# Attention and feed-forward on one core: third batch by DMA, other group cuts, x and output stores moved to GpSimd

## The chip, the cores and the metric

The kernel runs on one core of one Trainium2 chip. The metric is the device time of a launch in microseconds (us), as the median of several runs. Engines are called PE (TensorE matmul; PEld is its weight load), DVE (VectorE), ACT (ScalarE), POOL (GpSimd) and SP (SyncE). A letter q after a name (SPq, ACTq) means the engine's sequencer, which issues DMAs.

## What is computed

The inputs are q, k and v of 8 batches, 8 heads, 576 positions and 64 values a head, and two weight matrices.

```python
rel = pos[:, None] - pos[None, :]
mask_plain = (rel >= 0) & (rel < 32)
mask_dil = (rel >= 0) & (rel < 128) & (rel % 4 == 0)
# heads 0-3 take mask_plain, heads 4-7 take mask_dil
attn = softmax(where(mask, q @ k.T / 8, -1e9))
x = (attn @ v) as [4608 tokens, 512]     # tokens in the order batch, position
h = x @ w_in                             # 512 -> 2048
out = (h * sigmoid(h)) @ w_out           # 2048 -> 512, float32
```

## The kernel before, in words

The two weight matrices stay in SBUF as float16. The two layers go through the 4608 tokens in groups: two of 256 tokens, then eight of 512. **Layer 1** (`layer1`, L892 to L905) is 16 steps a group, one for each 128 rows of the hidden layer: four matmuls into a PSUM tile h, a tanh on ACT (th, L901), and the gate on DVE (gT, L903). **Layer 2** (`layer2`, L925 to L946) makes four steps of four matmuls for each 128 tokens into a PSUM tile y; ACT copies y to an output tile ob (L938, two buffers), and the ACT queue stores it (L939). The last 128 tokens are split in two, with one piece stored from SP (L946).

**Attention** works batch by batch. Scores (`scores`, L620 and L632) are computed transposed, by blocks of queries and a band of keys, exponentiated on ACT (L641, L645) and masked on DVE (L650). In the first batch the mask is added by matmuls against the identity (L620). `av` (L677 to L681) multiplies by v, with a column of ones that gives the sum, and DVE divides.

Scores need k and q with the head's 64 values on the partitions. There are two ways to that.

- *PE path*, batches 0 to 2 (`PEB = 3`): raw k and q are loaded from POOL's queue, cast to float16 on the way (nat; `issue_first`, `issue_nat` L124), and transposed on PE (L544, L521, L535; for batch 0 L557, L567, L582, L594). For batches 1 and 2, DVE or ACT first pairs the heads (`paired`, L652), and both copy the results out of PSUM (L510, L512).
- *DMA path*, batches 3 to 7: POOL issues a cast of k and of q into a DRAM scratch (kq_s, `issue_cast` L141), and SP issues four DMA transposes from it (`issue_turn`): two of the plain heads into nat (L155) and two of the dilated heads into kqT (L158). The plain ones read overlapping windows: 2304 rows of 128 values, one row at each step of 64, so that each value comes twice.

v is loaded from POOL too: vraw for dilated heads (two DMAs, L165) and vp for plain ones (one DMA of many small rows, L178).

The result x is needed transposed as well. For batches 0 to 2 (`PEX = 3`) PE transposes it into xA (L722, L733). For later batches SP stores it to a DRAM scratch x_s, in four DMAs a batch (oP L696, oD L715), and then transposes a whole group by DMA into xA or one of three rotating tiles xR (L450). Which group waits for which batch is in `need`: the batch of the group's last token.

**The order of the work** is fixed when the program is built. The class `Plan` holds a clock, the time at which each engine comes free, and rings of PSUM tiles. A loop (L990 on) takes at each moment a step that the plan holds ready, from three lists: attention, layer 1, layer 2. Layer 1 may be at most one group ahead of layer 2. What a step costs on an engine and when loads land (`AT_...`, `LOAD_US`, the numbers in the `yield` lines) are constants by hand. Every engine runs its own instructions in the order in which they were emitted.

`loads_gen` (L424 to L438) emits a batch's loads of the DMA path. POOL first copies one column of the previous batch's kqT (fence, L427), and, from batch 5 on, one of the x of two batches before (L429); each copy waits for that transpose to land. Then come vraw, vp and the casts. `turn_gen` emits the four transposes, `group_gen` the one of x, when all four stores of a batch are out (`stored`).

At the start, loads leave POOL in the order of `ORDER`: k0 and r0 are the rest of batch 0's k, q and v, v0 its plain v, w0a to w3 pieces of w_in, o0 to o3 pieces of w_out, d1, p1, r1, v1 the loads of batch 1 (dilated and plain k and q, vraw, vp). `third_batch` then emits raw loads of batch 2, its v, and the casts of batch 3. Eight matmuls of zeros (L192) run first on PE.

Of the kernel before, what the change touches and what calls it, by code (L numbers as in the profile page):

```python
# [16 lines left out]
def kernel(  # L17
# [9 lines left out]
    nc = tc.nc  # L27
# [17 lines left out]
    GROUPS = [(0, GT // 2), (GT // 2, GT // 2)] + [(t, GT) for t in range(GT, NT, GT)]  # L45
# [4 lines left out]
    PEB = 3  # L50
    PEX = 3
    GA = 4
    XR = 3
    NA = GA * GT
    BIG = 32768.0
    ORDER = "k0 r0 w0b v0 w0a w1 w2 w3 d1 p1 o0 r1 o1 o2 o3 v1".split()
    LOAD_US = {"w": 2.57, "o": 2.57, "d": 3.2, "p": 3.0, "r": 2.3, "v": 2.57, "k0": 2.2, "r0": 1.0, "v0": 2.3, "w0a": 1.3, "w0b": 1.3}
    AT_W0 = 11.4
# [18 lines left out]
    xA = cpool.tile([P, HP, GA * GT], F16, name="xA")  # L77
# [13 lines left out]
    NW = HN * S  # L91
# [7 lines left out]
        key: cpool.tile([MA, HP // 2, DIL, 2, D], F16, name=f"pair_{key}")  # L99
        for key in ("k", "q", "rest")  # L100
# [38 lines left out]
    def issue_cast(b):  # L139
        for i, src in enumerate((k, q)):  # L140
            nc.gpsimd.dma_start(  # L141
                out=kq_s[b][i].rearrange("(n p c) -> p n c", c=512, p=144),
                in_=src[b].rearrange("h s d -> (h s d)").rearrange("(n p c) -> p n c", c=512, p=144),
            )

    def issue_turn(b, n):
        i = n % 2
        flat = kq_s[b][i]
        if n < 2:
            if b < PEB + 2 and i == 0:  # L150
                nc.gpsimd.memset(kq_plain(b)[0][:, :LEAD], 0.0)
            win = bass.AP(tensor=flat.tensor, offset=flat.offset, ap=[[D, NW], [1, P]])
            dst = kq_plain(b)[i]
            dst = dst[:, LEAD:] if i == 0 else dst
            nc.sync.dma_start_transpose(out=dst[:, None, :], in_=win)  # L155
        else:
            rows = flat[HN * S * D :].rearrange("(n c) -> n c", c=DIL * D)
            nc.sync.dma_start_transpose(out=kqTs[b % 2][:, i], in_=rows)  # L158
# [29 lines left out]
    warm = vraws[1].rearrange("p a h r d -> p (a h r d)")  # L188
    nc.vector.memset(warm[:, :GT], 0.0)
    y_warm = ps_y.tile([P, GT], F32, tag="y", name="y_warm")  # L190
    for n in range(8):
        nc.tensor.matmul(y_warm, warm[:, :P], warm[:, :GT], start=True, stop=True)  # L192
    nc.vector.memset(warm[:, GT:], 0.0)
# [67 lines left out]
    def third_batch():  # L261
        for n in range(2, PEB):
            issue_nat(n, 0, H)
        issue_vraw(2)
        issue_vp(2)
        issue_cast(PEB)
        yield "DMA", 0.0
# [12 lines left out]
    class Plan:  # L280
        def __init__(self):
# [3 lines left out]
            self.free = {"ACT": 5.7, "DVE": 6.6}  # L285
# [75 lines left out]
    AT_DIL = {0: 6.1, 1: AT["d1"], 2: t2 + 7.0}  # L361
    AT_PLAIN = {0: 9.3, 1: AT["p1"], 2: t2 + 7.0}
    AT_VRAW = {0: 10.1, 1: AT["r1"], 2: t2 + 8.6}
    AT_VP = {0: 11.4, 1: AT["v1"], 2: t2 + 11.4}
    AT_CAST = t2 + 18.0
# [37 lines left out]
    turned = {b: Step(None, 0.0) for b in range(PEB, B)}  # L403
    groups = {g: Step(None, 0.0) for g in range(NG)}

    def x_of(g):
        t0, n = GROUPS[g]
        return xA[:, :, t0 : t0 + n] if t0 < NA else xRs[g % XR]

    def turn_gen(b):  # L410
        for n, us in enumerate((3.0, 3.0, 1.5, 7.5)):
            issue_turn(b, n)
            yield "DMA", us
# [7 lines left out]
    def start_turn(b):  # L421
        plan.push(turned[b], turn_gen(b), plan.now)

    def loads_gen(b):  # L424
        last = max(b - 1, PEB)
        for i in range(2):
            nc.gpsimd.tensor_copy(fence[:, i : i + 1], kqTs[last % 2][:, i, 1, HN * M - 1 :])  # L427
        if b - 2 >= PEX:
            nc.gpsimd.tensor_copy(fence[:, 2:3], x_of(first_of[b - 2])[:, HP - 1, GT - 1 :])  # L429
# [4 lines left out]
        yield "DMA", 9.0  # L434
        v_in[b].done = plan.now
        if b > PEB:
            yield "DMA", 4.5
# [9 lines left out]
    def group_gen(g):  # L447
        t0 = max(GROUPS[g][0], PEX * S)
        n = sum(GROUPS[g]) - t0
        nc.sync.dma_start_transpose(  # L450
            out=x_of(g)[:, :, GT - n :], in_=x_s[t0 : t0 + n]
        )
        yield "DMA", 6.0
        b = need[g]
        if g == first_of[b] and b + 2 < B:
# [10 lines left out]
    def attention(b):  # L466
# [21 lines left out]
        def k_plain(i, hp, j):  # L488
# [3 lines left out]
            c = LEAD + (2 * hp + i) * S + QB * j - W - i  # L492
            return kW[r, c : c + P]

        def q_plain(i, hp, j):
# [3 lines left out]
            c = (2 * hp + i) * S + QB * j - i  # L499
# [185 lines left out]
        def av_p(ring, j):  # L685
# [7 lines left out]
            if not pe_x and parts[j // 3] == 3:  # L693
                j = j // 3 * 3 + 2
                rows = x_s[b * S : (b + 1) * S, : HN * D].rearrange("(j p) c -> p j c", p=QB)
                nc.sync.dma_start(  # L696
                    out=rows[:, j - 2 : j + 1],
                    in_=oP[:, j - 2 : j + 1].rearrange("p j h d -> p j (h d)"),
                )
                yield "DMA", 3.0  # L700
                stored(b)

        def av_d(ring, ab, r):
# [8 lines left out]
            if not pe_x and parts[2 + ab] == DIL:  # L712
                t0 = b * S + ab * DIL * MH
                rows = x_s[t0 : t0 + DIL * MH, HN * D :].rearrange("(m r) c -> m r c", r=DIL)
                nc.sync.dma_start(out=rows, in_=oD[:, ab].rearrange("p r h d -> p r (h d)"))  # L715
                yield "DMA", 3.0
                stored(b)
# [24 lines left out]
        if b == 0:  # L742
            order = [
                ("TA", 1, "q"), ("TA", 0, "q"), ("V", 0), ("TD", 3), ("TS", 1), ("TS", 0),
                ("TD", 0), ("TA", 0, "k"), ("TD", 2), ("TD", 1), ("TA", 1, "k"), ("S", 3),
                ("TR",), ("S", 4), ("S", 6), ("S", 0), ("S", 1), ("D", 0, 1), ("P", 1), ("S", 5),
                ("D", 0, 0), ("D", 0, 2), ("V", 1), ("P", 0), ("S", 2), ("P", 3), ("P", 2),
                ("D", 1, 1), ("P", 4), ("D", 0, 3), ("P", 5), ("XP", 0), ("XP", 1), ("D", 1, 2),
                ("XD", 0), ("D", 1, 0), ("XP", 4), ("D", 1, 3), ("XP", 5), ("XP", 2), ("XD", 1),
                ("XP", 3), ("M",), ("B",),  # L750
            ]
        elif pe_path:
            order = [
                ("N", "k"), ("TD", 3), ("TD", 0), ("TD", 2), ("V", 0), ("TD", 1), ("N", "rest"),
                ("TA", 1), ("N", "q"), ("S", 3), ("TA", 0), ("TB", 0), ("TB", 1), ("D", 0, 1),
                ("D", 0, 0), ("S", 4), ("D", 0, 2), ("S", 0), ("P", 1), ("S", 1), ("D", 0, 3),
                ("P", 2), ("P", 0), ("XP", 0), ("XP", 1), ("S", 5), ("S", 6), ("XD", 0), ("V", 1),
                ("D", 1, 3), ("XP", 2), ("S", 2), ("D", 1, 2), ("D", 1, 0), ("D", 1, 1), ("P", 3),
                ("XP", 3), ("P", 4), ("XD", 1), ("P", 5), ("XP", 4), ("XP", 5),
            ]  # L760
        else:
            order = [
                ("S", 2), ("S", 0), ("P", 1), ("S", 3), ("S", 4), ("S", 1), ("S", 5), ("P", 0),
                ("V", 0), ("P", 5), ("P", 3), ("D", 0, 3), ("V", 1), ("P", 4), ("P", 2),
                ("D", 1, 1), ("D", 1, 3), ("D", 0, 1), ("D", 0, 2), ("D", 1, 2), ("D", 1, 0),
                ("D", 0, 0),
            ]
            if pe_x:
                order.insert(order.index(("D", 0, 0)), ("XP", 0))
                order.insert(order.index(("D", 0, 0)), ("XP", 1))  # L770
                order.insert(order.index(("D", 0, 2)), ("XP", 2))
                order.insert(order.index(("D", 0, 2)), ("XP", 3))
                order.insert(order.index(("D", 1, 0)), ("XP", 4))
                order.insert(order.index(("D", 1, 0)), ("XP", 5))
                order += [("XD", 0), ("XD", 1)]
        for key in order:
# [9 lines left out]
            elif kind == "TA" and b == 0:  # L786
                st = Step(
                    lambda ring, a=a: trans_a0(ring, *a), 0.36, rings,
                    [AT_PLAIN[0]],
# [18 lines left out]
            elif kind == "S":  # L808
                if not pe_path:
                    deps = [turned[b]]  # L810
# [104 lines left out]
    def layer2(g, l1s):  # L915
# [3 lines left out]
        def l2(ring, tb, f4, c0, c1):  # L919
# [15 lines left out]
            ob = o32.tile([P, c1 - c0], F32, tag="ob", bufs=2, name=f"ob_{g}_{tb}_{c0}")  # L935
            if c0 == 0:
                yield "ACT", 0.08 + (c1 - c0) / 1200
                nc.scalar.activation(ob, y, AF.Copy, scale=0.5)  # L938
                nc.scalar.dma_start(out=rows[:, c0:c1], in_=ob)  # L939
# [41 lines left out]
    LOOK = 8  # L981
    LIM_ATT = 1.1
    LIM_PAIR = 0.4
    LIM_L1 = 1.8
    SIDE = 0.9
    NEAR = 1.0
    SPARE = 6
# [80 lines left out]
```

The softmax here doesn't subtract the row's maximum and nothing guards it: scores larger than these inputs give would overflow.

## Time and profile before

| What | us |
|---|---|
| median of 6 runs | 313.15 |
| lowest, highest | 311.62, 316.82 |
| the profiled execution | 315.64 |
| its span, first instruction to last | 313.9 |
| busy: PE, DVE, ACT, POOL | 298.6, 195.9, 164.6, 54.7 |
| L925 (layer 2) on PE | 137.8 |
| L892 (layer 1) on PE, xR and xA | 77.6, 62.0 |

The page gives for each engine its busy time and its share of the span. The span is cut in 40 slices of about 7.85 us; a digit is a slice's busy share in tenths, and PEclk the clock that was granted to PE, in tenths. Matmuls are pipelined, and the profile counts one from its entry to its modelled end, so they overlap: x560 of 379 ns each are 134.3 us of busy time. A line of the waits view reads: who waited, for whom, microseconds in total, how many times, the longest. The chain of work follows the last instruction back to what released it each time; in its order of time a piece has a start, a length and what it was. A DMA is issued by an engine's queue and lands later; "DMA xR<-x_s" is the time from issue to landing.

### The profile page before, as it was taken

How to read it: one execution, taken by the hardware profiler on the slowest of the kernel's cores; microseconds unless marked ns; L12 is line 12 of the kernel's file. 1: busy time of each engine (PE TensorE's matmuls, PEld its weight loads, DVE VectorE, ACT ScalarE, POOL GpSimd, SP SyncE). 2: the span in 40 equal slices, each digit the busy share in tenths (PEclk: the TensorE clock that was granted, in tenths of full speed). 3: DMA queues.
4: the chain of work that ended last, by engine and by line, in shares of the span. 5: the costliest groups of instructions: out<-in, count | busy, mean ns of one | idle time of the engine just before them, and what ended most of it. 6: DMA issues, size and time to landing. Idle time of an engine off the chain costs nothing.

```text
span 313.9 us, 6177 instructions
## 1 busy us (share of the span) xinstructions
PE 298.6 (95%) x2402; PEld 155.1 (49%) x2402; DVE 195.9 (62%) x498; ACT 164.6 (52%) x318; POOL 54.7 (17%) x86
## 2 busy tenths in 40 slices
PE   6689989999999999999899979998999999999995
PEld 2469755555544545454455434544454444444444
DVE  6299997799768917773688347853885255455000
ACT  7488862767564627543653356434644355455111
POOL 8755732002800014000500050000000000000000
PEclk9599999999999999999999999999999999999999
DMA  8999999998999659989899969974114510000122
GB/s 107 178 198 193 202 191 197 212 173 167 152 207 209 152 148 162 198 182 214 103 194 220 195 104 199 222 177 103 50 57 124 114 36 33 33 33 2 69 98 70
DMA packets 107382, 44.55 MB, mean 142 GB/s; under 512 B 73304, under 2 KB 102872, under 8 KB 107352
## 3 DMA queue, kind: packets, MB, share of 16 engines
q0 software_dynamic: 48528, 19.86, 52.4%
q1 hardware_dynamic: 53496, 14.91, 25.1%
q10 hardware_dynamic: 5328, 9.37, 8.5%
q8 instruction: 19, 0.31, 0.4%
q14 instruction: 11, 0.09, 0.1%
HBM read 39.81 MB, written 18.28 MB: 185 GB/s over the span
## 4 chain that ended last, share of the span: by engine, by line
PE 74%; DMA 10%; DVE 8%; ACT 3%; SPq 2%; issue 1%; POOL 1%; ACTq 0%; DVEq 0%; POOLq 0%
PE h L892 33%; PE y L925 31%; DMA xR<-x_s 6%; PE s L632 2%; DMA x_s<-oD 2%; PE av_d L677 2%; DMA nat<-in_q_dram 2%; DVE oD L681 2%; SPq L158 2%; PE av_p L677 2%; DVE gT L903 2%; DVE probs L650 1%; ACT probs L641 1%; ACT ob L938 1%; DVE rcps L680 1%
## 5 line engine op out<-in xcount | busy, mean ns | idle before, releaser
L925 PE MATMUL y<-w_out,gT 128*128 128x512 f16 (+1 forms) x592 | 137.8, 373 | 0.0
L901 ACT ACTIVATE th<-h 128x512 f32<-128x512 f32 (+1 forms) x160 | 88.9, 557 | 82.4 <-PE h L892 71.2
L903 DVE SCALAR_TENSOR_TENSOR gT<-th,h 128x512 f16<-128x512 f32 (+1 forms) x160 | 99.2, 628 | 50.1 <-ACT th L901 49.6
L892 PEld LDWEIGHTS <-w_in 128*128 128x128 f16 x640 | 59.1, 97 | 56.6 <-issue 5.8
L925 PEld LDWEIGHTS <-gT 128*128 128x128 f16 x592 | 55.1, 98 | 57.5
L892 PE MATMUL h<-xR,w_in 128*128 128x512 f16 x320 | 77.6, 379 | 4.1 <-DMA xR<-x_s 4.1
L892 PE MATMUL h<-xA,w_in 128*128 128x512 f16 (+1 forms) x320 | 62.0, 336 | 0.0
L938 ACT ACTIVATE ob<-y 128x512 f32<-128x512 f32 (+1 forms) x36 | 21.3, 591 | 42.6 <-PE y L925 42.6
L641 ACT ACTIVATE probs<-s 128x768 f16<-128x768 f32 (+2 forms) x32 | 24.7, 772 | 11.7 <-PE s L632 9.8
L677 PEld LDWEIGHTS <-probs 128*128 128x128 f16 x448 | 21.9, 98 | 16.2 <-DVE probs L650 3.0
L681 DVE TENSOR_TENSOR oD<-av_d,rcps 72x256 f16<-72x256 f32 x64 | 26.9, 421 | 2.2
L650 DVE TENSOR_TENSOR probs<-probs,mask_p 128x768 f16<-128x768 f16 x21 | 11.5, 551 | 22.6 <-ACT probs L641 22.6
L681 DVE TENSOR_TENSOR oP<-av_p,rcps 96x256 f16<-96x256 f32 x48 | 20.2, 421 | 1.6
L427 POOL COPY fence<-kqT 128x1 f16<-128x1 f16 x10 | 1.9, 201 | 93.9 <-DMA kqT<-kq_s 93.9
L645 ACT ACTIVATE probs<-s 128x384 f16<-128x384 f32 (+2 forms) x38 | 17.2, 477 | 1.1 <-PE s L632 1.1
L677 PE MATMUL av_d<-vd,probs 128*128 128x65 f16 x256 | 15.3, 195 | 1.3 <-DVE oD L681 0.6
L945 DVE TENSOR_SCALAR ob<-y 128x128 f32<-128x128 f32 x1 | 0.3, 292 | 20.6 <-ACT ob L943 20.6
L680 DVE RECIPROCAL rcps<-av_p 96x4 f32<-96x4 f32 x48 | 8.3, 172 | 7.3 <-PE av_p L677 7.3
L677 PE MATMUL av_p<-vp,probs 128*128 128x65 f16 x192 | 12.0, 194 | 0.3
L680 DVE RECIPROCAL rcps<-av_d 72x4 f32<-72x4 f32 x64 | 11.0, 171 | 2.1 <-PE av_d L677 2.1
L165 POOL DMA_DIRECT2D vraw<-in_v_dram x16 | 11.2, 705 | 5.4 <-DVE rcps L680 2.3
L650 DVE TENSOR_TENSOR probs<-probs,mask_d 128x576 f16<-128x576 f16 (+1 forms) x23 | 11.6, 512 | 0.1
(93 smaller groups left out, 153.9 us busy)
## 6 DMA issues: line engine op xcount, KB each, us to landing
out_dram<-ob ACTq DMA_DIRECT2D x35, 256.0 KB, 2.8
kq_s<-in_k_dram POOLq DMA_DIRECT2D x5, 576.0 KB, 9.4
kq_s<-in_q_dram POOLq DMA_DIRECT2D x5, 576.0 KB, 12.3
vp<-in_v_dram POOLq DMA_DIRECT2D x7, 384.0 KB, 7.6
w_out<-in_moe_w_out_dram POOLq DMA_DIRECT2D x4, 512.0 KB, 10.9
vraw<-in_v_dram POOLq DMA_DIRECT2D x8, 224.0 KB, 5.6
w_in<-in_moe_w_in_dram POOLq DMA_DIRECT2D x3, 512.0 KB, 9.5
x_s<-oP SPq DMA_DIRECT2D x10, 144.0 KB, 3.7
```

What stands on the lines that cost most here:

```text
L165: nc.gpsimd.dma_start(out=vraw[p0 : p0 + m1 - m0, ab].rearrange("p h r d -> p h (r d)"), in_=src[m0:m1],)
L641: nc.scalar.activation(p2, both[:, :, :n], AF.Exp, scale=scale)
L645: nc.scalar.activation(p2[:, i], sp[i][:, :n], AF.Exp, scale=scale)
L650: nc.vector.tensor_tensor(p2, p2, mk, ALU.mult)
L677: nc.tensor.matmul(a[:, i, : D + 1], lhs(i), rhs(i), start=True, stop=True)
L680: nc.vector.reciprocal(rcp[:n], a[:n, :, D : D + 1])
L681: nc.vector.tensor_tensor(o, a[:n, :, :D], rcp[:n, :, None].broadcast_to([n, HN, D]), ALU.mult)
L892: nc.tensor.matmul(h[:, :w], w_in16[:, c, f * P : (f + 1) * P], x_g[:, c], start=(c == 0), stop=(c == HP - 1),)
L901: nc.scalar.activation(th[:, :w], h[:, :w], AF.Tanh, scale=0.5)
L903: nc.vector.scalar_tensor_tensor(gTs[g][:, f, :w], th[:, :w], 1.0, h[:, :w], ALU.add, ALU.mult)
L925: nc.tensor.matmul(y, gTs[g][:, f, tb * P : (tb + 1) * P], w_out16[:, f, c0:c1], start=(f == 0), stop=(f == NFF - 1),)
L938: nc.scalar.activation(ob, y, AF.Copy, scale=0.5)
```

## The change

The diff has these parts. Numbers in the planner (`AT_...`, `LOAD_US`, `LIM_...`, the written-out `order` lists of attention steps, which are permutations) change too and are cut here.

- Groups: 256, 256, 512, 128, then six of 512 from token 1152 on, then one of 384; eleven groups.
- `PEB = 2`: batch 2 takes the DMA path for k and q. Its x is still transposed on PE (`PEX = 3`). Its casts are emitted ahead of its v.
- The scratch of the plain heads holds two heads side by side: k and q are each cast by two DMAs with rows of 64 values and one DMA for the dilated heads. A plain transpose now reads 1152 rows.
- The four stores of a batch's x leave from POOL; SP keeps the transposes.
- The stores of groups 0 and 1 leave from POOL; ob has four buffers.
- The plan counts SP and POOL as engines, and keeps the readiness of plain and dilated heads apart.
- The order of the first loads.
- Dummy matmuls of 128 columns fill places where the plan holds PE idle between 5.5 and 18 us; the PSUM ring y is held until then.
- The pair tiles lie in xR's memory.

```diff
-    GROUPS = [(0, GT // 2), (GT // 2, GT // 2)] + [(t, GT) for t in range(GT, NT, GT)]
+    BT = 2 * S
+    GROUPS = [(0, GT // 2), (GT // 2, GT // 2), (GT, GT), (2 * GT, BT - 2 * GT)]
+    GROUPS += [(t, min(GT, NT - t)) for t in range(BT, NT, GT)]
...
-    PEB = 3
+    PEB = 2
...
-    ORDER = "k0 r0 w0b v0 w0a w1 w2 w3 d1 p1 o0 r1 o1 o2 o3 v1".split()
+    ORDER = "k0 w0a v0 r0 p1 w0b w1 w2 w3 d1 r1 o1 o0 o2 o3 v1".split()
...
-    NW = HN * S
+    NW = HP // 2 * S
...
     def issue_cast(b):
         for i, src in enumerate((k, q)):
+            flat = kq_s[b][i]
+            for hp in range(HP // 2):
+                nc.gpsimd.dma_start(
+                    out=flat[hp * S * P : (hp + 1) * S * P].rearrange("(s i d) -> s i d", i=2, d=D),
+                    in_=src[b, 2 * hp : 2 * hp + 2].rearrange("i s d -> s i d"),
+                )
             nc.gpsimd.dma_start(
-                out=kq_s[b][i].rearrange("(n p c) -> p n c", c=512, p=144),
-                in_=src[b].rearrange("h s d -> (h s d)").rearrange("(n p c) -> p n c", c=512, p=144),
+                out=flat[HN * S * D :].rearrange("(n p c) -> p n c", c=512, p=144),
+                in_=src[b, HN:].rearrange("h s d -> (h s d)").rearrange("(n p c) -> p n c", c=512, p=144),
             )
...
-            win = bass.AP(tensor=flat.tensor, offset=flat.offset, ap=[[D, NW], [1, P]])
+            win = flat[: NW * P].rearrange("(n c) -> n c", c=P)
...
+        issue_cast(PEB)
         issue_vraw(2)
         issue_vp(2)
-        issue_cast(PEB)
...
-        for n, us in enumerate((3.0, 3.0, 1.5, 7.5)):
+        for n, us in enumerate((4.0, 3.5, 1.0, 1.0) if b == PEB else (1.9, 1.9, 1.8, 1.8)):
+            yield "SP", us
             issue_turn(b, n)
-            yield "DMA", us
+            if n == 2:
+                turned["p", b].done = plan.now
+        yield "DMA", 3.0
...
-                nc.sync.dma_start(
-                    out=rows[:, j - 2 : j + 1],
-                    in_=oP[:, j - 2 : j + 1].rearrange("p j h d -> p j (h d)"),
-                )
-                yield "DMA", 3.0
-                stored(b)
+                data = oP[:, j - 2 : j + 1].rearrange("p j h d -> p j (h d)")
+                store(rows[:, j - 2 : j + 1], data)
...
+        def store_gen(rows, data):
+            yield "POOL", 0.8
+            nc.gpsimd.dma_start(out=rows, in_=data)
+            yield "DMA", 2.5
+            stored(b)
...
-            ob = o32.tile([P, c1 - c0], F32, tag="ob", bufs=2, name=f"ob_{g}_{tb}_{c0}")
+            ob = o32.tile([P, c1 - c0], F32, tag="ob", bufs=4, name=f"ob_{g}_{tb}_{c0}")
...
-                nc.scalar.dma_start(out=rows[:, c0:c1], in_=ob)
+                (nc.gpsimd if g < 2 else nc.scalar).dma_start(out=rows[:, c0:c1], in_=ob)
...
         if pick is None:
+            if plan.t < WARM:
+                if 5.5 < plan.t:
+                    nc.tensor.matmul(
+                        y_warm[:, :P], warm[:, :P], warm[:, :P], start=True, stop=True
+                    )
+                plan.t += 0.056
+                continue
```

Counted in the two programs, PE has 704 layer-1 matmuls for 640, 48 transposes of k and q fewer (24 of L544, 16 of L521, 8 of L535), and 79 dummy matmuls of 128 columns more. The order of POOL's queue in the changed program is, for batches 5 to 7: four stores of x of batch b - 2 (two oP, two oD), the two or three fence copies, two vraw, one vp, six casts. In it the four output stores of groups 0 and 1 stand behind vp of batch 2 and ahead of the fence for batch 3.

## The prediction

> **What bounds the kernel now.** I read the engine shares and the slices first, then stages by window, then who waited for whom, then the chain in order of time, then the timelines of SP and POOL.
>
> ```profile
> PE 298.6 (95%) x2402; PEld 155.1 (49%) x2402; DVE 195.9 (62%) x498; ACT 164.6 (52%) x318; POOL 54.7 (17%) x86
> PEclk9599999999999999999999999999999999999999
> ```
>
> TensorE looks full, and from the third slice on its clock is whole. But busy counts a matmul's way through the array, so I price the work itself. The chain ends in one unbroken run:
>
> ```profile
> 288.87 21.64 PE y L925 x116
> ```
>
> It holds 84 matmuls of 512 columns and 32 of 256, so 100 whole ones: 0.2164 us each. Both layers together are 1152 whole ones (rows of L892: 320 + 192 + 128/2; of L925: 560 + 32/2): **249.3 us that no order can shorten**. The first layer-1 matmul starts at 22.30 us, the last matmul ends at 310.3, the span is 313.9. The attention work left after 22.30 I price from the chain: 392 P·V matmuls at 30 ns (16 in 0.48), 392 score matmuls at 24 ns (20 in 0.48), 96 transposes of k and q at 43 ns (24 in 1.19 less 0.16 for the way through the array), 64 of x at 40 ns: 11.8 + 9.4 + 4.1 + 2.6 = 27.9 us. So of the 288.0 us between, 288.0 - 249.3 - 27.9 = **10.8 us are waiting**. Where:
>
> ```profile
> 31.30:55.00 23.70, 22.50 (x284) 15.01 (x282) 20.47 (x66) 14.44 (x36) 10.69 (x13) 1.00 1.50 196
> 55.00:80.00 25.00, 24.90 (x255) 13.66 (x254) 21.85 (x57) 17.87 (x35) 3.06 (x5) 1.00 1.20 181
> 140.00:225.00 85.00, 80.60 (x625) 38.48 (x623) 52.37 (x126) 41.58 (x75) 9.76 (x16) 1.00 0.93 164
> 240.00:311.00 71.00, 70.49 (x342) 33.14 (x340) 24.07 (x36) 27.81 (x48) 0.00 (x0) 1.00 0.21 62
> ```
>
> (Columns: window, length, busy of PE, PEld, DVE, ACT, POOL, clock, DMA share, GB/s.) The two clear stretches are 31 to 80 us, with VectorE at 86% (42.3 of 48.7), and 140 to 225, where PE is idle 4.4 us. The second has a name:
>
> ```profile
> PE h L892 <- DMA xR<-x_s: 4.1, 3, 2.3
> POOL fence L429 <- DMA xR<-x_s: 8.0, 2, 4.7
> 171.68 1.33 SPq L158
> 173.10 3.92 DMA x_s<-oD
> 177.04 6.00 DMA xR<-x_s
> 183.08 1.89 PE h L892 x8
> ```
>
> Layer 1 waits three times for a group's x: 4.1 us. The chain shows why: the last store of x leaves SP behind a transpose of k and q, lands 3.9 us later, and the x transpose takes 6.0. POOL waits for the same landing before it loads the next batch.
>
> **What the Trainium skill says.** "TensorE: Matmul & The Clock Gate", Part 1: the clock is at half until about 3.4 us of sustained work, and falls back after an idle window. The trace agrees: the second slice has 5 tenths, after PE idled from 7.8 to 10.5 us. "DMA: Bandwidth & Descriptors", Specifications: under 512 B a transfer is read-modify-write. The trace of before has 128 B writes only into SBUF (vp), so it cannot tell for DRAM. The same page, "Queues, rings and completion order": a ring is consumed in order, and an engine takes rows in turn; so a store moved to POOL's queue stands behind the casts there. Trace: the landings of POOL's DMAs are in order of issue throughout.
>
> **Third batch on the DMA path.** Removed on PE: 24 + 16 + 8 = 48 transposes (half of L544, L521, L535) x 43 ns = 2.1 us, all on the bounding engine: **-2.1**. Its copies leave DVE and ACT: three pair copies, 1.4 us, eight td copies / 2 = 2.1, ta and tb copies about 3.5: 7 us of the 31-to-80 stretch where VectorE is at 86%. What that returns is unknown: nothing, or at most about 3 us of the waits there. I take **-1.3**. Added: two casts and four transposes on DMA. The casts stand where the raw loads of that batch stood (landed 51.3 to 55.8 us); mine come to about 58, the transposes to about 66. Its first scores come after layer 2 of the first two groups and most of layer 1 of the third, about 72 us: hidden by some 6 us. If that cover goes, each us late is a us lost, once.
>
> **Plain halves of the scratch.** A transposed window held every row twice; now two heads lie side by side, so 1152 rows for 2304. One such transpose takes SP 3.16 us (median); half saves about 1.6, twice a batch: 3.2. Price: a plain half is written in 2304 packets of 128 B for 288 of 1 KB. Bounds for a packet's pace: 128 B into SBUF (vp, 3072 packets between landings 4.2 us apart: 1.35 ns) and the 1 KB cast (576 in 3.2 to 3.6 us: 5.9 ns). I take the low one: 3.1 us for 1.6, twice: +3.0. Loads to landed transposes now take 26.6 us (183.7 to 210.3): 26.6 - 3.2 + 3.0 = 26.4. That runs beside about 33 us of matmul per batch (x landed at 150.2, 183.0, 216.3): **0**, with 6.6 us of cover.
>
> **Groups cut at 1152.** Groups from 1664 on begin 128 tokens later than a batch's x was needed before (1664 for 1536), and the last has 384. 128 tokens are 249.3/36 = 6.9 us of slack, more than the largest wait (2.3). **x stores on POOL** take four DMAs from SP, so its transposes and the stores no longer hold each other. Queued behind a waiting store on POOL are the fence and loads of the next batch; they waited for that x anyway. Ahead of it are three v loads and six casts: about 1.4 + 1.4 + 6 x 0.85 = 7.9 us of issue, for 4.4, and about 19 us to land. P stores may land 2 to 3 us later for it; the last D stores come about when the casts end. Against that the third batch starts the chain later: loads of batch 3 stand behind four output stores, at about 71 us, so its k and q are ready at 97, for 85 before. That eats slack at the first two groups. x waits: 4.1 to 1.0, **-3.1** (from -4.1 to +2).
>
> **Output stores from POOL, four buffers.** The first four leave POOL after vp, 65 us or so; ACT loses four issues of 0.34 us and the one 2.0 us wait of L901 for a buffer. ACT is half idle: **0**. The fifth store's buffer is free by then (76 us). With two buffers, the late stores would stall ACT.
>
> **Load order.** w0a comes first, but the four loads p1 (3.1 us of landings) stand ahead of w0b. Stepping through before's landings: w0b 22.3, w1 24.9, w2 27.4, w3 29.95 us, for 16.6 to 26.9. Layer 1 of the first group can then end only at 29.95 + 4 x 0.43 = 31.7. PE has 16 h steps, 24 transposes, one score set by then, 8.4 us; before, 20 h steps and a transposed piece, 8.9 us, by 31.3. 0.4 later with 0.5 less done: **+0.9** (0 to +2.5). The first h step may come as late as 23 without loss, so the warm-up matmuls and the reordered first batch gain nothing beyond a whole clock: **0**.
>
> **Small group of 128 tokens.** 64 more matmuls and weight loads of 128 columns, 60 ns for 54, and 16 more tanh and gate steps: **+0.4**.
>
> Sum: -2.1 - 1.3 - 3.1 + 0.9 + 0.4 = -5.2 us. The profiled run took 315.64 us, 313.9 of it the span, so 1.7 around it; after it I expect a span of 308.7 and 310.4. That run lay 2.5 above the median of 313.15, so on the median: **308.0 us**.
>
> **Rivals.** (a) *Every wait goes*: x waits vanish (-4.1), relief of VectorE returns 3: -2.1 - 3.0 - 4.1 + 0.4 + 0.4 = -8.4, 304.7 us. For it: the slack of 6.9 us. Against it: the later start of the chain. (b) *The wait moves*: batch 3 and 4 are late by what 3 and 5 were, w_in costs 2 and relief gives nothing: -2.1 - 0.7 + 2.0 + 0.4 = -0.4, about 312.7 us. For it: w3 lands 3.1 us later while PE has nothing else. (c) *Slower: 128 B writes to DRAM*. Beyond (6.6/2 + 3.1)/2304 = 2.8 ns a packet, twice vp's pace, the chain from loads to transposes exceeds the 33 us per batch and becomes the bound. Midway between the bounds, 3.6 ns, a half takes 8.3 us: chain 26.4 + 2 x 5.2 = 36.8, 3.8 us over, in the four rounds of batches 4 to 7: +15.2, less 2.1 and 1.3, plus 1.3: about 326 us. For it: the skill's sentence. Against it: nothing in the trace shows it.
>
> **How the numbers follow.** Main case 0.58, own range 305 to 311.4; (a) 0.15; (b) 0.12; (c) 0.15. Half a per cent, 1.6 us, is about what a measurement of this kernel can tell from no change. Faster by more: main and (a), 0.73; within: (b), 0.12; slower: (c), 0.15. The range leaves out (c) and a little of (a): 302.5 to 313.
>
> **What would show it.** Right: the wait of layer 1 for xR at 1 us or less; casts' plain halves landing within 4 us each; a new wait of h for w_in before 31.7 us, 1 to 2 us; VectorE below 86% between 31 and 80 us. Wrong: scores waiting for nat or kqT, POOL's fence on kqT ending later than its fence on x (then c), or scores of the third batch waiting at 72 us.

## The result, and the profile after

The changed kernel takes **315.63 us** (median of 17 runs, 311.84 to 322.02); the kernel before, measured beside it, 312.52 (36 runs). The ratio is 1.0077, with a 95% interval of 1.0049 to 1.0105: about 2.4 us slower, where 5 us faster was forecast. A ratio here leaves out, on both sides, runs more than 1.5% above the fastest of their kernel, so it can differ from that of the medians. The profiled execution took 315.96 us, with a span of 313.9, the same as that of before.

The shares and the clock, from the page of the changed kernel:

```profile
PE 299.8 (95%) x2498; PEld 160.4 (51%) x2498; DVE 197.6 (63%) x507; ACT 163.6 (52%) x326; POOL 101.5 (32%) x132
...
PEclk9999999999999999999999999999999999999999
```

The clock is now whole from the second slice on (by the trace from 5.7 us, for 14.5 before): the dummy matmuls do what they are for. POOL's busy time has nearly doubled; it issues the casts in six pieces, the stores of x and four output stores.

The same four stretches as before the change (columns as there):

```profile
31.00:55.00 24.00, 23.11 (x276) 16.27 (x274) 21.55 (x65) 14.19 (x34) 14.32 (x16) 1.00 1.59 190
55.00:80.00 25.00, 25.00 (x185) 12.14 (x184) 15.40 (x30) 14.75 (x27) 7.49 (x11) 1.00 1.31 135
140.00:225.00 85.00, 84.06 (x688) 41.59 (x685) 62.92 (x159) 45.94 (x82) 28.84 (x36) 1.00 1.16 169
240.00:311.00 71.00, 70.09 (x355) 34.46 (x353) 21.39 (x36) 26.19 (x48) 0.00 (x0) 1.00 0.14 51
```

Two things that the forecast wanted are there. From 55 to 80 us DVE is busy 15.4 us for 21.85, and PE has no pause. From 140 to 225 PE is idle 0.9 us for 4.4: the wait of layer 1 for xR is gone. In its place, in the waits view:

```profile
POOL out_dram L953 <- ACT ob L952: 18.4, 3, 9.8
...
PE s L647 <- DMA nat<-kq_s: 3.4, 2, 2.5
...
PE h L906 <- DMA xA<-x_s: 1.2, 1, 1.2
...
PE h L906 <- DMA w_in<-in_moe_w_in_dram: 1.0, 1, 1.0
```

The first scores of batch 3 wait for their transposed k and q, and the rest of that chain is late behind them. PE's timeline shows the two places (start, length, what, and in brackets the idle time before it and who ended it):

```profile
30.51 3.67 PE L906 MATMUL h<-xA,w_in 128*128 128x256 f16 x32 [1.03 <-DMA w_in<-in_moe_w_in_dram]
...
96.27 0.52 PE L647 MATMUL s<-nat 64*128 64x96 f16 x16 [2.47 <-DMA nat<-kq_s]
```

Back from there one comes to POOL's timeline:

```profile
53.35 0.56 POOL L953 DMA_DIRECT2D out_dram<-ob  x1 [1.67 <-ACT ob L952]
...
61.03 0.54 POOL L953 DMA_DIRECT2D out_dram<-ob  x1 [6.96 <-ACT ob L952]
71.39 0.54 POOL L953 DMA_DIRECT2D out_dram<-ob  x1 [9.82 <-ACT ob L952]
71.92 0.20 POOL L441 COPY fence<-kqT 128x1 f16<-128x1 f16 x1
73.13 0.19 POOL L441 COPY fence<-kqT 128x1 f16<-128x1 f16 x1 [1.01 <-DMA kqT<-kq_s]
```

The fourth output store holds POOL until 71.4 us. Behind it stands the fence, and its second copy waits on: the last transpose of batch 2 lands at 73.1 us, where the forecast had about 66. Only then do batch 3's loads start. Two suspects: the *place* of the stores in POOL's order, or their *packets* beside the transposes.

### The profile page after: what moved, and what is told of

Read it like the earlier page. It is cut to its first block, busy times and chain, and to the rows that moved or that the text cites. A ratio compares the mean times of both kernels' runs of the same rounds, so it can differ in the third digit from the quotient of the medians.

```text
span 313.9 us, 6434 instructions
## 1 busy us (share of the span) xinstructions
PE 299.8 (95%) x2498; PEld 160.4 (51%) x2498; DVE 197.6 (63%) x507; ACT 163.6 (52%) x326; POOL 101.5 (32%) x132
## 3 DMA queue, kind: packets, MB, share of 16 engines
q1 hardware_dynamic: 40672, 10.19, 22.9%
## 4 chain that ended last, share of the span: by engine, by line
PE 73%; DMA 15%; POOL 5%; DVE 2%; ACT 2%; issue 1%; SPq 1%; ACTq 0%; POOLq 0%
PE y L939 35%; PE h L906 31%; DMA w_in<-in_moe_w_in_dram 6%; DMA nat<-kq_s 5%; DMA kq_s<-in_q_dram 3%; PE s L647 2%; PE av_d L692 2%; PE av_p L692 2%; POOL nat L134 1%; DMA kqT<-kq_s 1%; DVE gT L917 1%; SPq L167 1%; ACT th L915 1%; POOL kq_s L146 1%; POOL w_in L244 1%
## 5 line engine op out<-in xcount | busy, mean ns | idle before, releaser
L917 DVE SCALAR_TENSOR_TENSOR gT<-th,h 128x512 f16<-128x512 f32 (+3 forms) x176 | 101.6, 585 | 67.7 <-ACT th L915 66.5
L939 PE MATMUL y<-w_out,gT 128*128 128x512 f16 (+1 forms) x592 | 140.5, 373 | 0.2 <-DVE gT L917 0.2
L915 ACT ACTIVATE th<-h 128x512 f32<-128x512 f32 (+3 forms) x176 | 90.7, 521 | 83.7 <-PE h L906 76.5
L906 PEld LDWEIGHTS <-w_in 128*128 128x128 f16 x704 | 64.0, 98 | 60.2 <-issue 5.2
L906 PE MATMUL h<-xR,w_in 128*128 128x512 f16 (+1 forms) x320 | 73.8, 368 | 0.1
L906 PE MATMUL h<-xA,w_in 128*128 128x512 f16 (+2 forms) x384 | 67.8, 317 | 4.2 <-DVE gT L917 1.6
L696 DVE TENSOR_TENSOR oD<-av_d,rcps 72x256 f16<-72x256 f32 x64 | 26.9, 421 | 2.2
L730 POOL DMA_DIRECT2D x_s<-oP x10 | 12.3, 1234 | 35.0 <-DVE oP L696 22.5
L146 POOL DMA_DIRECT2D kq_s<-in_q_dram x12 | 22.3, 2552 | 0.7 <-DMA w_out<-in_moe_w_out_dram 0.7
L696 DVE TENSOR_TENSOR oP<-av_p,rcps 96x256 f16<-96x256 f32 x48 | 20.2, 420 | 1.6
L660 ACT ACTIVATE probs<-s 128x288 f16<-128x288 f32 (+2 forms) x42 | 19.1, 481 | 1.9 <-PE s L647 1.1
L146 POOL DMA_DIRECT2D kq_s<-in_k_dram x12 | 16.4, 1644 | 0.0
L150 POOL DMA_DIRECT2D kq_s<-in_q_dram x6 | 15.5, 2578 | 1.2 <-DMA w_out<-in_moe_w_out_dram 1.2
## 6 DMA issues: line engine op xcount, KB each, us to landing
w_out<-in_moe_w_out_dram POOLq DMA_DIRECT2D x4, 512.0 KB, 10.8
```

The source lines that it names most:

```text
L146: nc.gpsimd.dma_start(out=flat[hp * S * P : (hp + 1) * S * P].rearrange("(s i d) -> s i d", i=2, d=D), in_=src[b, 2 * hp : 2 * hp + 2].rea ...
L150: nc.gpsimd.dma_start(out=flat[HN * S * D :].rearrange("(n p c) -> p n c", c=512, p=144), in_=src[b, HN:].rearrange("h s d -> (h s d)").re ...
L660: nc.scalar.activation(p2[:, i], sp[i][:, :n], AF.Exp, scale=scale)
L696: nc.vector.tensor_tensor(o, a[:n, :, :D], rcp[:n, :, None].broadcast_to([n, HN, D]), ALU.mult)
L730: nc.gpsimd.dma_start(out=rows, in_=data)
L906: nc.tensor.matmul(h[:, :w], w_in16[:, c, f * P : (f + 1) * P], x_g[:, c], start=(c == 0), stop=(c == HP - 1),)
```

## The experiments

Times are medians, ratios are to the kernel before on the same chip, with a 95% interval. All edits are to the changed kernel unless said otherwise.

### The kernel before, again

> The kernel before, unchanged, profiled once more. The first profile was of an execution of 315.64 us, 3.1 above the median of 36 runs (312.52). Theory A (the baseline's waits were over-read): a typical execution has a span near 310.8 us and layer 1 waits for xR clearly less than 4.1 us, 2 us or less. Theory B (the waits were typical and the change really removed them, but paid more elsewhere): again about 4 us of waiting for xR.

317.66 us, span 315.9:

```profile
PE h L892 <- DMA xR<-x_s: 4.3, 2, 3.6
```

The waits for x came again, but in an execution 3.5 us above the median of the 43 runs beside it (314.17). That does not tell what a usual one has; two more profiles below do.

### Output stores back on ACT

```diff
-                (nc.gpsimd if g < 2 else nc.scalar).dma_start(out=rows[:, c0:c1], in_=ob)
+                nc.scalar.dma_start(out=rows[:, c0:c1], in_=ob)
```

> The changed kernel with the stores of the first two groups issued from ACT again; the order of all other instructions is the same, and four buffers stay. Theory A (third batch's transposes and v loads share the DMA engines, and the late batch 3 stalls PE at its first scores): the store's queue is only one more sharer, within 1 us of the changed kernel (about 315). Theory B (POOL, held by the four stores, starts batch 3 late): the fence for batch 3 passes several us before 73.5 us, the wait of the scores for nat near 94 us goes, 2 to 4 us faster (about 312).

312.4 us, ratio 0.996 (0.9934 to 0.9986): 1.2% under the changed kernel. The last transpose of batch 2 lands at 68.7 us for 73.1, and the wait for nat at 93 us is gone. A new stall stands at 61 us. ACT's timeline, then PE's:

```profile
59.15 0.60 ACT L952 ACTIVATE ob<-y 128x512 f32<-128x512 f32 x1 [0.27 <-PE y L939]
61.55 0.34 ACTq L953 DMA_DIRECT2D out_dram<-ob  x1
61.99 1.08 ACT L915 ACTIVATE th<-h 128x512 f32<-128x512 f32 x2 [2.24 <-DMA nat<-kq_s]
```

```profile
63.36 1.96 PE L906 MATMUL h<-xA,w_in 128*128 128x512 f16 x8 [1.66 <-DVE gT L917]
```

The tile ob is ready at 59.75, yet ACT issues its store only at 61.55. The profile names the landing of the first transpose of nat (61.48) as the releaser, though ACT does not read nat. The trace tells why. A DMA reports its landing on a semaphore, a counter with a number; SP's and ACT's DMAs share a small set of them (108 and 112 to 118), and in this program the store was given 112, the one on which that transpose was still out. ACT waits on 112, is released at 61.50, and only then issues. So the stall comes from how the numbers fell in this program, not from SP's issuing at that time. The tanh behind the store starts late, and PE waits 1.7 us.

Theory B's number came. That its mechanism, POOL held by the four stores, is not the main one is shown by the last two experiments.

### Stores of x back on SP

```diff
-            nc.gpsimd.dma_start(out=rows, in_=data)
+            nc.sync.dma_start(out=rows, in_=data)
```

> The changed kernel with the stores of x issued from SP again, at the same places of the plan. Theory A (the stores wait in POOL's ring behind the casts, 5 us to land, and this makes the x transposes late): landing falls to about 3.5 us, layer 1 no longer waits at 125 us, 1 to 2 us faster. Theory B (SP's transposes and stores hold each other, as before): kqT is issued later in every batch, waits of scores for kqT appear, 1 to 4 us slower.

316.2 us, ratio 0.9975 (0.9931 to 1.0018); its 22 runs spread from 309.8 to 319.7, so that the ratio rests on seven of them. The profiled execution, one of the long ones (317.95 us), has a wait for nat of 5.0 us at 93 us, and one for xR of 0.7. So with the stores of x off POOL the loss can still come, in the same place. What sets the short executions apart was not looked into, and neither theory is decided.

### Third batch back on PE

```diff
-    PEB = 2
+    PEB = 3
```

with the emission order and the load times of that batch as before.

> The changed kernel with the third batch on the PE path again (48 transposes on PE, raw loads, casts of batch 3 after its v, as before). Theory A (the third batch on DMA starts the chain of batch 3 late): the wait of 2.5 us for nat near 94 us goes, first scores of batch 3 have their data some 10 us earlier, and although PE has 2.1 us more to do the kernel is 1 to 3 us faster than the changed one (313 to 315). Theory B (the loss is elsewhere: load order, groups, x stores): it is 1 to 3 us slower than the changed one (317 to 319).

322.56 us, ratio 1.0263 (1.0207 to 1.0319). The wait for nat is there here too (3.1 us, now at 172 us), and one of 3.2 us for w_in. Putting the third batch back does not win the loss back. But the planner lays out the whole order anew with such an edit, and its constants were set for the other form, so this is not the price of the part.

### No output stores of the first two groups

```diff
-                (nc.gpsimd if g < 2 else nc.scalar).dma_start(out=rows[:, c0:c1], in_=ob)
+                if g >= 2:
+                    nc.scalar.dma_start(out=rows[:, c0:c1], in_=ob)
```

> The changed kernel with the four output stores of the first two token groups left out altogether (those 512 output rows are not written; all the arithmetic stays). Theory A, that the loss is made by these stores in GpSimd's queue (they stand before the fence on batch 2's transposes and their packets lie beside those transposes): the transposes of batch 2 land at about 68 to 69 us instead of 73.1, the loads of batch 3 start by 69.5, the first scores of batch 3 wait for nat 0.5 us or less at 93 to 98 us, and, since no store on ACT is held either, the time is 310.5 to 311.5 us, 0.985 to 0.99 of the changed kernel. Theory B, that the chain of batch 2 and 3 is late for other reasons (the casts and v of that batch, the x stores on GpSimd): nat still waits 2 us or more at 93 to 98 us and the time is within 0.4% of 315.6 us. Theory C, that only the place on a queue matters and the 1 us stall that stores on ACT brought at 61 us is noise: the same as with the stores on ACT, 312.4 us.

311.21 us, ratio 0.9949 (0.9926 to 0.9973). POOL's fence, with both stores and their traffic gone:

```profile
66.03 0.19 POOL L441 COPY fence<-kqT 128x1 f16<-128x1 f16 x1 [14.10 <-DMA kqT<-kq_s]
67.00 0.19 POOL L441 COPY fence<-kqT 128x1 f16<-128x1 f16 x1 [0.78 <-DMA kqT<-kq_s]
```

Six us earlier than in the changed kernel, and no wait for nat. Theory A's number came: the four stores cost 1.0077 - 0.9949 = 1.28%, or 4.0 us (4.4 by the medians). Against the same four stores on ACT it is 1.0077 - 0.9960 = 1.17%, 3.7 us.

### Both kinds of stores on their old queues

The edits of the second and third experiment together.

> Output stores back on ACT and the stores of x back on SP, the rest as changed. If moving the stores of x to GpSimd is what takes away the waits of layer 1 for xR (the forecast's 3.1 us), these waits come back: 2 to 4 us in 140 to 225 us and 314 to 315.5 us. If the later group boundaries (1664 for 1536) and the shorter transposes do it, the waits stay under 1.5 us in all and the time is that of the stores on ACT alone, 312 to 312.8 us. If the stores of x on GpSimd themselves delay the next batch's loads, it is faster than that, 311 us.

312.92 us (14 runs), ratio 1.0023 (0.9991 to 1.0055). In its profile PE never waits for xR, though the stores of x are on SP. But that execution is a short one (311.34), and short executions of the kernel before have none of these waits either, as two profiles below show. So it is not shown that the other edits (group cuts, shorter transposes) are enough without POOL's queue.

### Only the third store on POOL

```diff
-                (nc.gpsimd if g < 2 else nc.scalar).dma_start(out=rows[:, c0:c1], in_=ob)
+                (nc.gpsimd if (g, tb) == (1, 0) else nc.scalar).dma_start(out=rows[:, c0:c1], in_=ob)
```

> Three of the first four output stores leave from ACT, and only the third, which ACT would have to issue at 60 us while SP issues the transposes of batch 2, leaves from GpSimd. Theory A with the reading that ACT's issue is held by SP's transposes: the 1.8 us stall at 61 us goes, GpSimd is not held to 71 us by the fourth store, batch 2's transposes land by about 70 us and nat's wait at 93 us stays under 1 us: 311 to 311.8 us. If one store on GpSimd is already enough to delay the transposes, or if the stall at 61 us moves to another store, it is 312.4 us or more.

311.33 us, ratio 0.9963 (0.9939 to 0.9987): as good as no stores, within the intervals. Its window from 55 to 80 us has no pause of PE, so the stall at 61 us is gone; here no store on ACT is given a semaphore on which another DMA is still out:

```profile
22.00:31.00 9.00, 7.04 (x86) 5.56 (x84) 7.47 (x22) 7.44 (x21) 3.57 (x6) 1.00 1.18 187
...
55.00:80.00 25.00, 25.00 (x173) 12.10 (x172) 15.36 (x30) 14.52 (x28) 8.02 (x12) 1.00 1.41 150
```

The expectation of transposes by 70 us was missed: they landed at 72.0, though the first one was issued 1.4 us later than in the changed kernel (51.6 for 50.2). Yet nat for batch 3 lands at 92.65, and its scores start at 95.27 without a wait.

### Output stores on ACT, loads in the old order

```diff
-    ORDER = "k0 w0a v0 r0 p1 w0b w1 w2 w3 d1 r1 o1 o0 o2 o3 v1".split()
+    ORDER = "k0 r0 w0b v0 w0a w1 w2 w3 d1 p1 o0 r1 o1 o2 o3 v1".split()
```

> Output stores on ACT as before, and the order of the first loads as before the change too (half of w_in after k, r and v; the four plain loads of batch 1 after w3). The forecast put the new load order at +0.9 us (0 to 2.5). If that is right and nothing hides it now that the wait for nat is gone: 0.9 us less than with the stores on ACT alone, 311.5 us, with no wait of h for w_in at 30 us. If the later w_in is paid for by a better start elsewhere (batch 1's k and q earlier): 312.4 us or up to 313.5.

321.87 us, ratio 1.0234 (1.0158 to 1.0311). A miss of both expectations: the planner set a different order for the whole kernel, and three waits for nat (3.0 us) came back. This tells nothing of the load order by itself.

### The kernel before, with the stores of x on POOL

Two edits to the kernel before (L696, L715 of its file):

```diff
-                nc.sync.dma_start(
+                nc.gpsimd.dma_start(
```

> The kernel before with one part of the change alone: the stores of x leave from GpSimd instead of SP. The forecast gave the waits of layer 1 for x as made by these stores standing behind SP's transposes, and took 3.1 us for their going. Theory A (the forecast's own): those waits in 140 to 225 us fall from about 4 us to 1 us or less and the time falls by what they cost on the median, 1.5 to 3 us, to 310 to 311.5 us. Theory B, that the group boundaries and the shorter transposes took the waits away and the queue of the stores matters little (with the other parts of the change the stores did as well on SP): within 0.3% of the kernel before. Theory C: GpSimd, held by its fence, issues the stores later than SP did: slower by 1 us or more.

312.14 us, ratio 0.9972 (0.9954 to 0.9991), and the runs lie close together (311.59 to 313.15). PE waits nowhere for xR, and the long executions, up to 317.39 us in the kernel before on that chip, are gone. So the mechanism that the forecast gave is right in the kernel before, and its worth is 0.28%, 0.9 us (0.3 to 1.4), or 1.2 us between the medians of all runs, not 3.1.

### The kernel before, twice more

> The kernel before, profiled once more, to see whether its waits of layer 1 for x are there in every execution. The two profiles so far lie 2.5 and 4.5 us above the median and show 4.1 and 4.3 us of them. If the waits are what sets a long execution apart from a short one, an execution near 311 to 313 us shows 0 to 2 us of them, and the forecast, which took 3.1 us for the waits and then 2.5 us again for the distance to the median, counted the same time twice. If they are in each, about 4 us also here.

> As the run before it, one more execution: the wait of layer 1 for x should go with the execution's distance from 311 us (theory of the double count), or be about 4 us whatever the time.

312.48 and 312.43 us. PE at the place where the first two profiles had up to 3.6 us of waiting, in the first and in the second:

```profile
180.69 1.89 PE L892 MATMUL h<-xR,w_in 128*128 128x512 f16 x8 [0.20 <-DMA xR<-x_s]
```

```profile
180.91 1.89 PE L892 MATMUL h<-xR,w_in 128*128 128x512 f16 x8
```

0.2 us and nothing. The waits for x are not in each execution of the kernel before: in these four profiles they are what sets the two long ones apart.

### No dummy matmuls

On top of the version with one store on POOL, `if 5.5 < plan.t:` becomes `if False:`.

> The changed kernel with only the third output store on GpSimd, and without the 70 small dummy matmuls that keep TensorE busy between 5.5 and 18 us. The forecast put the whole clock that they bring at nothing, since w_in lands late anyway: then 311.3 us, the same as with them, though the first attention steps run at half clock from 8 to 14 us. If the earlier first step of layer 1 is worth what it looks (1 us): 312.3 us.

310.64 us (7 runs), ratio 0.9914 (0.9882 to 0.9946): the best version seen, faster than both kernels; its interval overlaps that of the version with the dummy matmuls. The same edit on the changed kernel with all its stores:

> The changed kernel without the 70 small dummy matmuls between 5.5 and 18 us, all stores as changed. The forecast put them at nothing. With one store on GpSimd their absence gave 310.6 for 311.3 us, on another chip, so not yet told apart. If TensorE's early work is what the wait for nat at 93 us swallows anyway: within 0.3% of 315.6 us. If the dummy matmuls themselves delay the start of something (the first loads' chain), 0.5 us or more faster than that.

318.37 us (6 runs), ratio 1.0205 (1.0164 to 1.0247): slower than with them. The two signs differ, and why was not settled.

### Place or packets: the fourth store, or the first three

```diff
+                (nc.gpsimd if (g, tb) == (1, 1) else nc.scalar).dma_start(out=rows[:, c0:c1], in_=ob)
```

> Only the fourth of the first four output stores leaves from GpSimd, the other three from ACT. GpSimd then still waits until about 71 us for that store's data before it comes to its fence on batch 2's transposes, but no store's packets of GpSimd's lie beside those transposes. If the wait in GpSimd's order is the loss: the fence ends at 71.5 us or later though the transposes land at about 69, nat is waited for 1 us or more at 93 us, and the time is 313.5 us or more. If it is the stores' traffic beside the transposes: as with all four on ACT, 312.4 us, with its stall at 61 us.

```diff
+                (nc.gpsimd if g < 2 and (g, tb) != (1, 1) else nc.scalar).dma_start(out=rows[:, c0:c1], in_=ob)
```

> The first three output stores leave from GpSimd, the fourth from ACT: GpSimd is held only until 61 us, and the packets of three stores lie beside batch 2's transposes. If the wait in GpSimd's order (the fourth store) is the loss: 311.3 us, as with the third alone. If the stores' traffic beside the transposes is: the transposes still land at about 73 us, nat is waited for 1.5 us or more, and the time is 314 to 315.6 us.

With the fourth alone 312.97 us, ratio 1.0008 (0.998 to 1.0037). With the first three 316.08 us, ratio 1.012 (1.0077 to 1.0164): the whole loss. POOL's timeline with the fourth alone:

```profile
71.61 0.58 POOL L953 DMA_DIRECT2D out_dram<-ob  x1 [20.09 <-ACT ob L952]
72.18 0.31 POOL L441 COPY fence<-kqT 128x1 f16<-128x1 f16 x2
```

POOL is held for 20 us, past the landing of the transposes (70.0); still the scores start at 93.91 without a wait, nat being there at 93.47. This execution is a short one (311.29; its 22 runs reach 316.32), so it does not show where the longer ones lose. With the first three, POOL is free at 61, and waits for the transposes:

```profile
72.39 0.19 POOL L441 COPY fence<-kqT 128x1 f16<-128x1 f16 x1 [11.22 <-DMA kqT<-kq_s]
74.72 0.19 POOL L441 COPY fence<-kqT 128x1 f16<-128x1 f16 x1 [2.15 <-DMA kqT<-kq_s]
```

and PE waits at the first scores of batch 3:

```profile
97.21 0.82 PE L647 MATMUL s<-nat 64*128 64x96 f16 x16 [3.86 <-DMA nat<-kq_s]
```

So it is mainly the packets. The place in the order is not free, since it takes up the slack to within half a us (0.6%, 1.8 us, above no stores at all, and 0.5% above all four stores on ACT), and the two prices do not add up: with both the loss is 1.28%. The time from the issue of batch 2's first transpose to the landing of its last goes with the stores: 16.1 us without any, 19.1 with all four on ACT, 19.6 and 20.4 with only the fourth or only the third on POOL, 22.9 in the changed kernel, 24.8 with the first three. The packet records of 55 to 72 us (a packet is here one record of the trace) show the same: a 256-byte packet of the transposes took 41 ns in the changed kernel and 55 with the first three stores on POOL, for 33 to 38 with one store there or none. A store leaves POOL's queue in packets of 4096 bytes, some 300 ns each then, ACT's in packets of 2048 bytes at 128 to 148.

Which property of these packets does it stays open. One is their size. The Trainium skill, "DMA: Bandwidth & Descriptors", Queues, rings and completion order, says that each DMA engine goes round the queues and drains a whole packet, there a group of descriptors, from one before it turns to the next; a transpose beside larger packets would then wait longer for its turn. The other is the time at which they move. On POOL the first two stores stand behind vp and land at 68.4 and 69.1 us, in the midst of the transposes; from ACT they had landed at 53.6 and 60.4. No run varied the one without the other.

## Why the prediction was wrong

**"Output stores from POOL, four buffers: 0" is the step that failed.** It priced the issue (ACT half idle) and the buffers, and named no cover for the transfers. Measured: 3.7 us against the same stores on ACT (1.17%), 4.0 against none (1.28%). The step placed the stores "after vp, 65 us or so". They are issued at 51, 53 and 61 us, and land behind vp at 68.4 to 70.6, in the stretch where SP moves batch 2's transposes. Those were forecast for "about 66" and landed at 70.7 and 73.1. The cover of "some 6 us" at 72 us was not the one that gave out: batch 2's own scores did not wait. The one after it did, since batch 3's loads are fenced on those transposes: first loads 73.7 for 71, k and q complete at 99.6 for 97, nat at 96.2, where PE had wanted it at 93.8. Not all of this comes over the fence: against the runs with only the third or only the fourth store on POOL, the loads of batch 3 start 1.1 and 1.3 us later, but nat lands 3.6 and 2.8 us later. The rest arises among batch 3's own casts and transposes, and why was not settled.

**"That run lay 2.5 above the median" counted the x waits twice.** The sum took 3.1 us of waits out of an execution of 315.64 us, then another 2.5 for its distance to the median. The two later profiles show that an execution of 312.4 us has none of these waits, so the distance and the waits are one thing. The step's mechanism was right: with the stores on POOL alone in the kernel before they are gone, and in the changed kernel's profile too, though two later profiles with the stores of x on POOL have one of 0.9 us (output stores on ACT) and one of 1.7 (without the dummy matmuls). But the size is 0.9 us, not 3.1.

**The other terms** can be read by counting PE's work by columns and calling the rest pause. In the changed kernel's trace the starts of neighbouring matmuls lie 216 ns apart with 512 columns and 56 with 128, so 384 columns take 160 ns, 2400 a us; the hand-over between matmuls falls to the pauses, and the 64-row score matmuls, which run in pairs, count half. By this count the attention work that the prediction put at 27.9 us is 23.3, so its 10.8 us of waiting were too few (about 19, with the hand-overs). On the left the mean of three executions without x waits (the two of before, and the one with the stores of x on POOL), on the right three of the changed kernel without the packets beside the transposes (no stores, only the third on POOL, only the fourth):

| | before, no x waits | changed, no nat wait |
|---|---|---|
| first layer-1 matmul at | 22.4 | 21.0 |
| attention work after it | 23.3 | 21.4 |
| pauses 22 to 31 us | 1.0 | 3.1 |
| 31 to 55 | 3.5 | 3.3 |
| 55 to 80 | 2.5 | 0.9 |
| 80 to 140 | 2.4 | 4.6 |
| 140 to 225 | 4.7 | 4.1 |
| last matmul ends, less its way through the array | 306.7 | 306.1 |

- *Third batch, -2.1 and -1.3*: right. 1.9 us less work, and 1.6 us less pause from 55 to 80, where DVE is relieved. From 31 to 55, where relief was also looked for, nothing came.
- *Scratch layout, 0*: right, and rival (c) is refuted. In a quiet stretch a cast of 1152 packets of 128 bytes lands every 0.95 us (0.83 ns a packet, under the low bound of 1.35). Of a price for writes under 512 B to DRAM, which the prediction feared, nothing shows.
- *Load order, +0.9*: right. Layer 1 begins 1.4 us sooner, then starves: from 22 to 31 us PE is busy 7.0 us of 9 in the version with one store on POOL. The kernel before with its stores of x on POOL has, in the same window:

```profile
22.00:31.00 9.00, 9.00 (x90) 8.08 (x90) 8.76 (x27) 7.60 (x22) 4.45 (x7) 1.00 1.37 198
```

  At 31 us these three have 260.7 us of work left, for 261.1, although their whole work is 1.9 less: about 1.5 us lost. All eight profiles that run the changed program up to there (with the stores moved later or not) have 260.0 on the mean, the five of the kernel before 261.0: 1.0 us lost. So the forecast's 0.9 is within the scatter. w3 landed at 30.46 us (forecast 29.95), the wait ended at 30.5 (forecast before 31.7).
- *Small group, +0.4*: too small for what happens from 80 to 140 us, 2.2 us more pause. Part of it is three short waits, for DVE's gate, that stand at the same places in each of these executions (by this count 0.33 us near 94, 0.71 near 116, 0.38 near 122; the profile's own gaps are some 0.16 shorter). In the version with one store on POOL, for one:

```profile
117.38 1.89 PE L906 MATMUL h<-xA,w_in 128*128 128x512 f16 x8 [0.55 <-DVE gT L917]
```

  The order runs layer 1 there for eight matmuls and eight more, and each pair of h tiles has to pass ACT and DVE first. The forecast looked for no new wait there. The rest of the 2.2 us is not settled.

Together, from the table: -1.9 - 1.6 + 1.5 + 2.2 - 0.6 (140 to 225) - 0.9 (x waits) = -1.3 us without the stores, where the run without them has -1.6 (ratio 0.9949); with their 4.0 us, +2.7, for a measured +2.4.

**Of what was to show it wrong**, "scores waiting for nat or kqT" came, but the bracket after it ("then c") named the wrong cause, and "slower" had been given to the 128-byte writes alone. All four signs of its being right came too (no wait for xR, a half's two casts landing within 2 to 3 us, a wait of 1.0 us for w_in, VectorE at 75% between 31 and 80 us): each looked at a term that had a price, none at the one put at nothing.

## What to carry to other kernels

A store that is moved to another queue still moves its bytes: ask which transfers it lies beside there, who is fenced on those, and how much slack the second link of that chain has, not only the first. When a profiled execution lies above the median, find what makes it long before taking waits out of it; if those waits are the difference, they must not be subtracted twice. One or two more profiles of the kernel before would have shown it. And when a profile names a releaser that the waiting engine does not read, look at the semaphore numbers in the trace: two DMAs may merely share one.

## What the runs showed of the hardware that was not expected

- A long wait of PE can cost more than itself. After the 3.9 us wait with the first three stores on POOL, the clock is at half for 3 us (the column before the last two is the clock):

```profile
97.00:100.00 3.00, 2.79 (x21) 1.35 (x21) 1.12 (x2) 1.57 (x3) 0.79 (x2) 0.50 0.71 155
```

  In the long execution of the kernel before, after its 3.6 us wait for x, likewise:

```profile
184.00:187.00 3.00, 2.07 (x5) 0.69 (x5) 0.00 (x0) 0.17 (x1) 1.60 (x4) 0.53 0.04 4
```

  That is up to 1.5 us more (an estimate: 3 us at half clock). The length from which it happens is not sharp. After the changed kernel's wait of 2.5 us the clock stayed whole (1.00 from 96 to 99 us); in the changed kernel without the dummy matmuls a wait as long was followed by half clock:

```profile
125.06 2.97 PE L906 MATMUL h<-xA,w_in 128*128 128x512 f16 x8 [2.54 <-DMA xA<-x_s]
...
125.70:129.10 3.40, 3.40 (x16) 1.48 (x15) 1.44 (x5) 1.19 (x2) 0.73 (x4) 0.50 0.73 143
```

  The Trainium skill, "TensorE: Matmul & The Clock Gate", Part 1, has the clock fall back after an idle window of about 3.4 us. The waits of 3.9 and 3.6 us fit that; the last one is shorter, and there the measurement decides. The prediction's example does not fit either: in the trace of before the clock went to half at 7.65 us, ahead of the pause from 8.0 to 10.5 to which the prediction gave it.
- SP's issuing of a transpose does not hold ACT's stores. In the changed kernel a store on ACT whose tile was ready at 86.24 us was issued at 86.27, while SP was issuing a transpose (85.21 to 86.81); with the fourth store on POOL the third left ACT as fast (ready 60.84, issued 60.87). Only in the two programs with all four output stores on ACT did the third wait, 1.8 and 1.3 us, and in both it had the semaphore of a transpose that was still out.
- An output store of the same 256 KB goes out in 4096-byte packets from POOL and in 2048-byte packets from ACT.
